# A fourth buffer for the weights' words, an operand zeroed in place, and another order of the first transfers, in a gated linear recurrence with a squared-ReLU network

## The chip, the core and the metric

The kernel runs on one core of a Trainium2 chip. The metric is the device time of one execution in microseconds, the median of several runs. Besides, one execution was recorded by the hardware profiler; all times of single instructions come from that one, and count from the start of its span. A core has five instruction streams that run side by side: PE (TensorE, matrix products), DVE (VectorE), ACT (ScalarE), POOL (GpSimd) and SP (SyncE). Each stream does its instructions strictly in order. SP, ACT and POOL can also issue DMA transfers between memory and the on-chip SBUF; the transfers share 16 DMA engines.

## What is computed

Two stages. The first is a gated recurrence with a complex gate for each of 4 sequences, 8 heads, 768 steps and head size 48; its output, regrouped to 3072 tokens of 384 numbers, goes through a two-layer network with squared ReLU.

```
mag = sqrt(a_re^2 + a_im^2);  scale = min(mag, 0.999) / (mag + 1e-6)
for t in range(S):
    new_re = ar * S_re - ai * S_im
    new_im = ar * S_im + ai * S_re
    S_re, S_im = new_re + outer(k[t], v[t]), new_im
    y[t] = q[t] @ S_re
h = maximum(x @ w_in, 0)          # x: y as (3072, 384); w_in: 384 x 2048
out = (h * h) @ w_out             # w_out: 2048 x 384
```

The weights w_in and w_out are stored as 64-bit floats, and the kernel itself turns them into 32-bit floats on the chip.

## The kernel before

The 3072 tokens are cut into 24 chunks of 128, and two chunks of different sequences form a group: 12 groups. For each group the kernel

- loads gates, queries and keys (`load_parts`, L492 to L511) into the one tile `raw` and the values (`load_values`, L518) into two of the four tiles `vt`. For each chunk b and each half hh of the partitions, `load_parts` issues one large transfer of the rows of three of the four head pairs (L503), and two or three small ones for the fourth pair, whose rows are spread over the 16 partitions that are left (L511; called gap transfers here);
- makes the operands (`make_operands`, 23 steps written o*group*.*step*). Steps 0 and 3 to 11 normalise the gate: o.0 squares (ACT), o.3 their sum (DVE), o.4 and o.5 inverse root and its square (ACT), o.7 a correction (DVE), o.8 to o.10 three scaled copies (ACT), o.11 the gates (DVE, L751 to L755). o.1 and o.2 copy the gate into `ab`, o.6 copies the queries. Step 22 (`grown_squared`, ACT, L764 to L767) and step 13 (`grow`, DVE, L771) form the running product of the gate's growth with a scan; the scan's second operand, `begun`, is a tile of zeros with six columns filled in. Then come the block steps 15 to 17, carries 18 and 19, the products 20, and 21, six small transfers from SBUF to SBUF (`last`);
- forms scores, state and outputs of chunk 0 (steps a*group*.*k*) and chunk 1 (b*group*.*k*), with PE, ACT and DVE. a.1 to a.4 turn the keys (PE) and copy them to `kt` (ACT), a.0 are the scores, a.5 the mask, a.6 the product with the values, a.8 the sum of keys and values, a.9 the new state;
- runs the two-layer network on the group (F, H, X, Y, Z, Q, R), and stores it (s).

Beside the first groups the weights are fetched in 16 blocks of 768 KB, eight of w_in and eight of w_out: f*i* issues the first half of block i on SP and j*i* the second half on POOL (blocks of w_out come whole, on SP), into one of three `words` buffers. D*i* decodes a block on DVE (five instructions, L587 to L596) and W*i* watches its range on ACT (two activations with their sums, L600 to L602). A buffer is free for the fetch three blocks on when D and W have read it. The three sums of the second weight (t0 to t2) take their place in the same ring later.

The order of the work on every engine is written out by hand: the string FRONT (L1072) is gone through token by token, and each token puts its instructions at the end of the streams that they belong to. So a token's place orders it against the others on the same stream alone: l0.0 (gates of group 0), v0, v1 (values of groups 0 and 1), f0, l0.1 (queries and keys of group 0, first half of the partitions; i0.1 the second, on POOL), f1, f2, ... stand in this order on SP. M0 loads ACT's table, M1 makes the mask from the tile `plain` on ACT and PE.

Ahead of FRONT, POOL sets constants: `ident`, `plain`, and zeros in the ends of `vt`, in `qk`, `last`, `prod`, the states, `kt` and `begun`.

Of the kernel before, what the change touches and what calls it, by code (L numbers as in the profile page):

```python
# [21 lines left out]
F32 = mybir.dt.float32  # L22
BF16 = mybir.dt.bfloat16
I32 = mybir.dt.int32
U32 = mybir.dt.uint32
AF = mybir.ActivationFunctionType
ALU = mybir.AluOpType
PSUM = bass.MemoryType.PSUM

P = 128  # L30
# [14 lines left out]
def gap_rows(hh, d):  # L45
    return slice(hh * ROWS + d, (hh + 1) * ROWS)
# [18 lines left out]
def w2_view(w):  # L65
    return w.rearrange("(fb p) m -> p fb m", p=P)
# [359 lines left out]
def quotient_path(ctx, tc, feat, vtok, w_in, w_out, w1, w2, out, n_seq, count):  # L426

    nc = tc.nc
    N, _, D, _, NP, C = feat.shape
    DM, FF = w_in.shape  # L430
# [6 lines left out]
    NFB = FF // P  # L437
    SEG = GC * NG
    E = SEG * C
    L = 8  # L440
    NB = C // L
    W = C + 2
# [4 lines left out]
    const = ctx.enter_context(tc.tile_pool(name="const", bufs=1))  # L447
    dec = ctx.enter_context(tc.tile_pool(name="dec", bufs=1))
    nrm = ctx.enter_context(tc.tile_pool(name="nrm", bufs=1))
    tmp = ctx.enter_context(tc.tile_pool(name="tmp", bufs=1))  # L450
# [10 lines left out]
    def rows(hh):  # L461
        return head_rows(hh, D)
# [7 lines left out]
    def pads(hh):  # L470
        return gap_rows(hh, D)
# [7 lines left out]
    def tt(out, in0, in1, op):  # L479
        nc.vector.tensor_tensor(out=out, in0=in0, in1=in1, op=op)  # L480
# [2 lines left out]
    raw = const.tile([P, 4, GC, NG, C], F32, name="raw")  # L483

    vt = [const.tile([C, DM + PAD], F32, name=f"vt{i}") for i in range(2 * GC)]
    for t in vt:
        nc.gpsimd.memset(t[:, DM:], 0.0)


    TWO_QUEUES = 3  # L490
# [1 line left out]
    def load_parts(gi, part=None, second=False):  # L492


        parts = [slice(A_RE, Q), slice(Q, V), slice(A_RE, V)][2 if part is None else part]
        queues = [nc.sync, nc.scalar if part == 0 else other if gi < TWO_QUEUES else nc.sync]
        if part != 0 and gi < TWO_QUEUES:
            queues[not second] = None
        for b, n in enumerate(groups[gi]):
            for hh, queue in enumerate(queues):  # L500
                if queue is None:
                    continue
                queue.dma_start(  # L503
                    out=raw[rows(hh), parts, b].rearrange("d x g t -> d x (g t)"),
                    in_=feat[n, hh, :, parts, 0:NG].rearrange("d x g t -> d x (g t)"))

                gap = raw[pads(hh), parts, b]
                rest = feat[n, hh].rearrange("(r g) x p t -> r x g p t", g=NG)[:, parts, :, NG]
                for i in range(min(gap.shape[1:3])):
                    at = (slice(None), i) if gap.shape[1] < NG else (slice(None), slice(None), i)  # L510
                    queue.dma_start(out=gap[at], in_=rest[at])  # L511
# [15 lines left out]
    nc.vector.memset(ones, 1.0)  # L527

    mask = const.tile([C, C], F32, name="mask")
    plain = const.tile([C, C], F32, name="plain")  # L530
    nc.gpsimd.memset(plain, 1.0)
    nc.gpsimd.affine_select(out=plain, in_=plain, pattern=[[-1, C]], compare_op=ALU.is_ge, fill=0.0,
                            base=0, channel_multiplier=1)
# [1 line left out]
    def turn_mask(step):  # L535
        if step == 0:

            nc.scalar.activation(out=sums[:, 0:1], in_=tiny, func=AF.Abs_reciprocal_sqrt)
            return
        nc.scalar.copy(out=mask.rearrange("p (j n) -> p n j", j=L),  # L540
                       in_=plain.rearrange("p (n j) -> p n j", j=L))
        turned = pm.tile([C, C], F32, tag="m", name="turned")
        nc.tensor.transpose(turned, mask, ident)
        nc.scalar.copy(out=mask.rearrange("p (j n) -> p n j", j=L),
                       in_=turned.rearrange("p (n j) -> p n j", j=L))
# [8 lines left out]
    qk_of = [const.tile([P, 4, GC, NG, W], F32, name=f"qk{i}") for i in range(2)]  # L554
    last = [const.tile([P, 4, GC, W], F32, name=f"last{i}") for i in range(2)]
    prod = [const.tile([P, 3, GC, NP], F32, name=f"prod{i}") for i in range(2)]
    for t in qk_of:
        nc.gpsimd.memset(t[:, :, :, :, C:W], 0.0)

    states = [[const.tile([P, 2, NP, ROWS], F32, name=f"state{b}{i}") for i in range(2)]  # L560
              for b in range(GC)]
    for t in last + prod + states[0] + states[1]:
        nc.gpsimd.memset(t, 0.0)
    kt = [const.tile([C, NP, P], F32, name=f"kt{i}") for i in range(2)]
    for t in kt:
        nc.gpsimd.memset(t, 0.0)

    sums = const.tile([P, NGR], F32, name="sums")
    ends = const.tile([P, NGR, SEG], F32, name="ends")
    begun = const.tile([P, E], F32, name="begun")  # L570
    nc.gpsimd.memset(begun, 0.0)
    sizes = const.tile([P, 2, 2 * NBLK], F32, name="sizes")
    nc.vector.memset(sizes, 1.0)
    tiny = const.tile([P, 1], F32, name="tiny")
# [30 lines left out]
    words_of = {}  # L605

    def block(i):

        return order[i] == "2", order[:i].count(order[i])

    def fetch(i, second=False):
        of_w2, j = block(i)
        f, fbs = slice(j * BLK, (j + 1) * BLK), slice(j * 2, (j + 1) * 2)
        if (w_out if of_w2 else w_in).dtype == F32:
            if second:
                return
            if of_w2:
                nc.sync.dma_start(out=w2[:, fbs], in_=w2_view(w_out)[:, fbs])
            else:
                for at, gs, src in w1_views(w_in, D, crossed=True):  # L620
                    nc.sync.dma_start(out=w1[at, gs, f], in_=src[:, :, f])
            return
        if i not in words_of:
            words_of[i] = dec.tile([P, E, 2], I32, name="words", bufs=3)
        words = words_of[i]
        if of_w2:
            nc.sync.dma_start(out=words.rearrange("p (k m) w -> p k (m w)", k=2),
                              in_=w2_view(w_out)[:, fbs].bitcast(I32))
        else:
            for at, gs, src in w1_views(w_in, D, crossed=True):  # L630
                if (at.start >= ROWS) != second:
                    continue
                (other if second else nc.sync).dma_start(
                    out=words[at].rearrange("p (g f) w -> p g (f w)", g=NG)[:, gs],
                    in_=src[:, :, f].bitcast(I32))
# [13 lines left out]
    def sum_weights(i):  # L649
        x, y = ((half[0][1], half[0][0]), (half[1][1], w2_sums[0] if i else None),  # L650
                (half[1][0], w2_sums[1] if i > 1 else None), (half[1][1], half[0][1]))[i]
        w2_sums.append(half[0][1] if i == 3 else
                       dec.tile([P, NFB // 2, DM // 2], F32, tag="words", name="w2_sum", bufs=3))
        tt(w2_sums[i], x, y, ALU.subtract)

    def factor(z):
# [17 lines left out]
    def make_operands(gi):  # L674
# [4 lines left out]
        tiles = {}  # L679
# [81 lines left out]


        def grown_squared():
            nc.scalar.activation(out=tiles["sq"][:, 0], in_=tiles["sq"][:, 1], func=AF.Square)  # L764
            at = tiles["sq"][:, 0].rearrange("p (s t) -> p s t", s=SEG)[:, :, 0]
            nc.scalar.copy(out=begun.rearrange("p (s t) -> p s t", s=SEG)[:, :, 0], in_=at)
            nc.scalar.mul(out=at, in_=at, mul=0.0)  # L767

        def grow():
            u, v = tiles["sq"][:, 0], tiles["sq"][:, 1]  # L770
            nc.vector.tensor_tensor_scan(out=v, data0=u, data1=begun, initial=0.0, op0=ALU.mult,  # L771
                                         op1=ALU.add)
            tt(r[:, K], r[:, K], v, ALU.mult)

# [267 lines left out]
    def outputs(i, r):  # L1042
# [27 lines left out]


    FRONT = (  # L1072
        "l0.0 M0 j0 v0 v1 f0 o0.0 l0.1 i0.1 o0.3 o0.1 o0.4 o0.5 o0.7 o0.2 M1 o0.8 D0 f1 j1 o0.9 "
        "o0.10 o0.6 o0.11 f2 j2 W0 W1 D1 o0.22 f3 j3 o0.12 W2 o0.13 o0.15 o0.14 f4 j4 W3 l1 i1 "
        "o0.16 W4 o0.17 D2 o0.18 o1.6 o0.19 f5 j5 o0.20 o1.0 W5 a0.1 o1.3 o0.21 o1.1 D3 a0.2 "
        "a0.3 o1.4 a0.4 a0.8 o1.5 o1.2 o1.7 f6 j6 b0.0 a0.9 o1.8 b0.1 b0.5 o1.9 b0.6 D4 b0.2 "
        "b0.3 b0.7 a0.0 b0.4 o1.10 W6 b0.8 o1.11 f7 j7 a0.5 o1.12 o1.22 a0.6 b0.9 o1.13 W7 v2 "
        "a0.7 o1.15 o1.14 g0 l2 i2 o1.16 F0.0 o1.17 F0.1 H0.0 D5 o1.18 F0.2 H0.1 o2.6 o1.19 f8 "
        "F0.3 H0.2 F0.4 H0.3 o1.20 o2.0 F0.5 H0.4 W8 a1.1 o2.3 o1.21 D6 a1.2 a1.3 o2.1 a1.4 "
        "a1.8 o2.4 o2.2 F0.6 D7 f9 H0.5 o2.5 a1.0 H0.6 a1.9 F0.7 a1.5 W9 f10 o2.7 a1.6 b1.1 "  # L1080
        "a1.7 D8 b1.0 o2.10 o2.8 H0.7 b1.5 o2.9 f11 b1.6 D9 b1.2 b1.3 b1.7 T0.0 b1.4 g1 W10 "
        "o2.11 T0.1 W11 f12 F1.0 D10 o2.12 o2.22 F1.1 H1.0 D11 T0.2 H1.1 f13 W12 F1.2 o2.15 "
# [61 lines left out]
    def ranges(step):  # L1144
# [33 lines left out]
        "R": outputs,  # L1178
        "s": store,
        "f": fetch,  # L1180
        "j": lambda i: fetch(i, True),
        "i": lambda gi, part=None: load_parts(gi, part, True),
        "D": weights,
        "W": lambda i: watch(words_of[i], i) if i in words_of else None,
        "t": sum_weights,
        "l": load_parts,
        "v": load_values,
        "M": turn_mask,
        "K": ranges,
    }  # L1190
# [65 lines left out]
```

## Time and profile before

| | |
|---|---|
| time, median of 5 runs | 707.14 us (705.84 to 707.90) |
| the profiled execution | 706.8 us, its span 705.1 us |
| PE busy | 618.9 us (88%) |
| DVE busy | 524.2 us (74%) |
| ACT busy | 386.2 us (55%) |
| POOL busy | 36.1 us (5%) |
| mean granted TensorE clock | 0.986 |
| moved by DMA | 47.75 MB |
| chain that ended last | PE 75%, DVE 14%, DMA 4%, ACT 3% |

The table's shares are means over the whole span. The page also cuts the span into 40 slices of 17.6 us and gives the busy share of each in tenths; there the start looks unlike the rest:

```profile
PE   0006489999889999999999999999999999999995
...
DVE  1899999999699786896785885995986976972120
...
DMA  6973634461333063061151051151240330110101
```

PE does nothing in the first three slices, about 53 us; DVE is almost empty in the first slice only; DMA is busiest in the second. The chain "that ended last" is followed backwards from the last instruction: at each step to what released it. SPq in a row is a transfer being issued by SP, and DMA a transfer under way.

### The profile page before, as it was taken

The page shows a single profiled execution, that of the slowest core. Times are in us where ns is not written, and L with a number is a line of the kernel's source. Part 1 is how long each engine was busy: PE and PEld are TensorE (multiplying, and loading weights), DVE is VectorE, ACT ScalarE, POOL GpSimd, SP SyncE. Part 2 cuts the span into 40 slices and gives each one's busy share as a digit, 9 for nine tenths or more (in the row PEclk, how much of TensorE's full clock was granted, in tenths as well). Part 3 has the DMA queues.
Part 4 walks back from the last instruction along what each step waited for, and adds up shares of the span by engine and source line. Part 5 has one row for each costly group of instructions (what it writes and reads, how often), then busy time and mean ns, then how long its engine had stood idle before and what let it go on. Part 6 is the DMA issues. An engine that isn't in the chain of part 4 may idle for free.

```text
span 705.1 us, 12510 instructions
## 1 busy us (share of the span) xinstructions
PE 618.9 (88%) x4955; PEld 544.4 (77%) x4955; DVE 524.2 (74%) x916; ACT 386.2 (55%) x684; POOL 36.1 (5%) x91
## 2 busy tenths in 40 slices
PE   0006489999889999999999999999999999999995
PEld 0005377776578898998999989989989989989895
DVE  1899999999699786896785885995986976972120
ACT  6638487754648547537457557366476476440330
POOL 6331200000000000000000000000000000000000
PEclk9999699999999999999999999999999999999999
DMA  6973634461333063061151051151240330110101
GB/s 166 191 136 70 143 78 144 143 111 43 68 74 64 6 94 71 2 125 39 29 113 23 29 113 24 52 94 20 75 80 11 84 77 5 29 23 2 29 1 28
DMA packets 44164, 47.75 MB, mean 68 GB/s; under 512 B 6016, under 2 KB 39104, under 8 KB 44096
## 3 DMA queue, kind: packets, MB, share of 16 engines
q1 hardware_dynamic: 41408, 41.35, 27.9%
q0 software_dynamic: 2208, 5.11, 3.7%
q8 instruction: 41, 0.67, 0.4%
q10 hardware_dynamic: 480, 0.39, 0.2%
q14 instruction: 27, 0.22, 0.1%
HBM read 36.18 MB, written 4.72 MB: 58 GB/s over the span
## 4 chain that ended last, share of the span: by engine, by line
PE 75%; DVE 14%; DMA 4%; ACT 3%; SPq 2%; issue 1%; DVEq 0%; ACTq 0%
PE h_ps L961 30%; PE o_ps L1038 26%; PE a_ps L872 7%; PE y L898 3%; DMA words<-in_moe_w_in_dram 3%; PE y L864 3%; PE add L919 3%; DVE pr L480 2%; DVE ab L480 2%; PE tp L879 2%; DVE room L480 1%; PE o_ps L977 1%; DVE qk L480 1%; DVE decoded L589 1%; DVE decoded L594 1%
## 5 line engine op out<-in xcount | busy, mean ns | idle before, releaser
L961 PE MATMUL h_ps<-x,w 128*128 128x256 f32 x1152 | 257.5, 384 | 6.8 <-DMA x<-x 6.8
L961 PEld LDWEIGHTS h_ps<-x,w 128*128 128x128 f32 x1152 | 220.3, 193 | 37.9 <-issue 6.0
L966 ACT ACTIVATE h<-h_ps 128x512 f32<-128x512 f32 x96 | 57.5, 599 | 103.7 <-PE h_ps L961 95.8
L1038 PE MATMUL o_ps<-w,h 128*128 128x192 f32 x640 | 111.1, 328 | 0.0
L1038 PEld LDWEIGHTS o_ps<-w,h 128*128 128x128 f32 x640 | 103.6, 190 | 1.8 <-issue 0.9
L480 DVE TENSOR_TENSOR pr<-ab 128x384 f32<-128x384 f32 (+2 forms) x168 | 66.4, 413 | 4.4 <-ACT ab L759 0.5
L967 ACT ACTIVATE h<-h 128x512 f32<-128x512 f32 x96 | 60.6, 631 | 3.0
L879 PE MATMUL tp<-ident,qk 128*128 128x128 f32 x120 | 22.0, 294 | 44.6 <-DVE qk L480 42.7
L480 DVE TENSOR_TENSOR a<-a_ps,mask 128x1024 f32<-128x1024 f32 x24 | 29.4, 1223 | 38.4 <-PE a_ps L872 38.4
L480 DVE TENSOR_TENSOR mix<-h 128x256 f32<-128x256 f32 x40 | 16.9, 421 | 53.7 <-ACT h L967 53.7
L1038 PE MATMUL o_ps<-w_sum,mix 128*128 128x192 f32 x320 | 55.9, 328 | 0.0
L1038 PEld LDWEIGHTS o_ps<-w_sum,mix 128*128 128x128 f32 x320 | 52.0, 190 | 1.1 <-DVE state L480 0.7
L879 PEld LDWEIGHTS tp<-ident,qk 128*128 128x128 f32 x120 | 13.6, 145 | 50.6 <-issue 43.8
L480 DVE TENSOR_TENSOR ab<-pr 128x192 f32<-128x192 f32 (+1 forms) x180 | 45.8, 276 | 4.6
L685 ACT ACTIVATE qk<-raw 128x768 f32<-128x768 f32 x24 | 36.7, 1531 | 16.3 <-DVE raw L480 8.8
L480 DVE TENSOR_TENSOR qk<-ab,qk 128x768 f32<-128x768 f32 x48 | 44.9, 956 | 0.9
L977 PE MATMUL o_ps<-w,h 128*128 128x384 f32 x128 | 42.3, 488 | 0.0
L872 PE MATMUL a_ps<-qk 48*128 48x128 f32 x576 | 39.8, 286 | 0.0
L872 PEld LDWEIGHTS a_ps<-qk 48*128 48x128 f32 x576 | 35.2, 193 | 4.2 <-issue 4.2
L685 ACT ACTIVATE ab<-raw 128x768 f32<-128x768 f32 x24 | 37.1, 1562 | 2.3 <-DVE qk L480 2.3
L480 DVE TENSOR_TENSOR room<-ab,carry 128x1344 f32<-128x1344 f32 x24 | 36.2, 1551 | 2.2 <-ACT carry L800 2.2
L977 PEld LDWEIGHTS o_ps<-w,h 128*128 128x128 f32 x128 | 24.1, 190 | 16.2 <-DVE w L480 0.7
(106 smaller groups left out, 804.3 us busy)
## 6 DMA issues: line engine op xcount, KB each, us to landing
raw<-in_feat_dram SPq DMA_DIRECT2D x40, 288.0 KB
words<-in_moe_w_out_dram SPq DMA_DIRECT2D x8, 768.0 KB
last<-qk SPq DMA_DIRECT2D x72, 64.5 KB
vt<-in_vtok_dram SPq DMA_DIRECT2D x24, 192.0 KB
out_dram<-o SPq DMA_DIRECT2D x24, 192.0 KB
raw<-in_feat_dram SPq DMA_DIRECT2D x120, 32.0 KB
words<-in_moe_w_in_dram POOLq DMA_DIRECT2D x8, 192.0 KB, 4.9
words<-in_moe_w_in_dram SPq DMA_DIRECT2D x8, 192.0 KB
```

Source lines behind the costliest of these rows:

```text
L480: nc.vector.tensor_tensor(out=out, in0=in0, in1=in1, op=op)
L685: nc.scalar.activation(out=out.rearrange("p c j n -> p c n j"), func=AF.Copy, in_=in_.rearrange("p c (n j) -> p c n j", j=L), **kwargs)
L864: nc.tensor.matmul(ys[p_ % 2][crossed(hh, p_), p_ // 2], lhsT=states[b][1 - c_seq % 2][rows(hh), c, p_], rhs=operand(c, p_, rows(hh)), sta ...
L872: nc.tensor.matmul(ps[:, hh, p_], lhsT=operand(2 + c, p_, rows(hh)), rhs=operand(c, p_, rows(hh)), start=(c == RE), stop=(c == IM))
L879: nc.tensor.transpose(tp[:, g], operands[gi][:, 2 + c, b, g, 0:C], ident)
L898: nc.tensor.matmul(tiles["y"][p_ % 2][crossed(hh, p_), p_ // 2], lhsT=v[:, at:at + ROWS], rhs=tiles["am"][:, hh, p_], start=(first and p_ ...
L919: nc.tensor.matmul(add[rr, c, p_], lhsT=kt[c][:, p_, rr], rhs=v[:, at:at + D], start=True, stop=True)
L961: nc.tensor.matmul(ps[:, j], lhsT=w1[:, g, (2 * f + j) * P:(2 * f + j + 1) * P], rhs=x_of[i][:, g], start=(g == 0), stop=(g == NG - 1))
L966: nc.scalar.activation(out=h, in_=h_ps[i, f], func=AF.Relu)
L967: nc.scalar.activation(out=h, in_=h, func=AF.Square)
L977: nc.tensor.matmul(o_of[i, b], lhsT=tokens_of(i, f, b)[:, j], rhs=w2[:, k], start=(k == 0), stop=(k == NFB - 1))
L1038: nc.tensor.matmul(to, lhsT=x(k)[:, j], rhs=factor(z)[:, 2 * k + j], start=(z in (0, 1, 3) and k == j == 0), stop=(k == KH // 2 - 1 and j ...
```

## The change

Five edits.

1. The ring of `words` (and of the weight sums) gets four buffers instead of three. Room for it comes from `begun`, which is no longer a tile of its own, and from `plain`, which now lies in the tile of the temporary `pr`.
2. `grown_squared` takes a half of the group's own tile `room` (`both[:, 0]`, read last by the gates) as `begun`. So POOL zeroes it once for every group, between the gates (L754) and ACT's copy into it (L766).
3. POOL's zeros for `qk`, `last`, `vt`, `kt`, `prod` and the states move from the start to a token M2, which stands on POOL between j1 and j2.
4. In l0.0 the gap transfers of chunk 1 (two that were SP's, two that were ACT's) go to POOL's queue.
5. FRONT's start changes. On SP the blocks 0, 1 and 2 now come ahead of the values: l0.0, f0, l0.1, f1, f2, v0, f3, v1, f4 instead of l0.0, v0, v1, f0, l0.1, f1, f2, f3, f4. Further on, o1.5 moves ahead of a0.4, and b0.2 ahead of b0.5 and o1.9.

```diff
-    for t in vt:
-        nc.gpsimd.memset(t[:, DM:], 0.0)
...
+                if part == 0 and b:
+                    queue = nc.gpsimd
                 gap = raw[pads(hh), parts, b]
...
-    plain = const.tile([C, C], F32, name="plain")
+    plain = tmp.tile([P, 4 * NP * D], F32, tag="pr", name="plain")[:, 0:C]
...
+            return
+        if step == 2:
+
+            for t in ([t[:, :, :, :, C:W] for t in qk_of] + last + [t[:, DM:] for t in vt]
+                      + kt + prod + states[0] + states[1]):
+                nc.gpsimd.memset(t, 0.0)
             return
...
-    begun = const.tile([P, E], F32, name="begun")
-    nc.gpsimd.memset(begun, 0.0)
...
-            words_of[i] = dec.tile([P, E, 2], I32, name="words", bufs=3)
+            words_of[i] = dec.tile([P, E, 2], I32, name="words", bufs=4)
...
-                       dec.tile([P, NFB // 2, DM // 2], F32, tag="words", name="w2_sum", bufs=3))
+                       dec.tile([P, NFB // 2, DM // 2], F32, tag="words", name="w2_sum", bufs=4))
...
         def grown_squared():
+            begun = tiles["both"][:, 0]
+            nc.gpsimd.memset(begun, 0.0)
...
-            nc.vector.tensor_tensor_scan(out=v, data0=u, data1=begun, initial=0.0, op0=ALU.mult,
+            nc.vector.tensor_tensor_scan(out=v, data0=u, data1=tiles["both"][:, 0], initial=0.0, op0=ALU.mult,
...
-        "l0.0 M0 j0 v0 v1 f0 o0.0 l0.1 i0.1 o0.3 o0.1 o0.4 o0.5 o0.7 o0.2 M1 o0.8 D0 f1 j1 o0.9 "
-        "o0.10 o0.6 o0.11 f2 j2 W0 W1 D1 o0.22 f3 j3 o0.12 W2 o0.13 o0.15 o0.14 f4 j4 W3 l1 i1 "
-        "o0.16 W4 o0.17 D2 o0.18 o1.6 o0.19 f5 j5 o0.20 o1.0 W5 a0.1 o1.3 o0.21 o1.1 D3 a0.2 "
-        "a0.3 o1.4 a0.4 a0.8 o1.5 o1.2 o1.7 f6 j6 b0.0 a0.9 o1.8 b0.1 b0.5 o1.9 b0.6 D4 b0.2 "
-        "b0.3 b0.7 a0.0 b0.4 o1.10 W6 b0.8 o1.11 f7 j7 a0.5 o1.12 o1.22 a0.6 b0.9 o1.13 W7 v2 "
+        "l0.0 M0 f0 j0 l0.1 i0.1 f1 j1 M2 f2 j2 v0 o0.0 o0.3 o0.1 o0.4 o0.5 o0.7 o0.2 M1 o0.8 "
+        "D0 o0.9 o0.10 o0.6 o0.11 W0 W1 D1 o0.22 f3 v1 j3 o0.12 W2 o0.13 o0.15 o0.14 f4 j4 W3 "
+        "l1 i1 o0.16 W4 o0.17 D2 o0.18 o1.6 o0.19 f5 j5 o0.20 o1.0 W5 a0.1 o1.3 o0.21 o1.1 D3 "
+        "a0.2 a0.3 o1.4 o1.5 a0.4 a0.8 o1.2 o1.7 f6 j6 b0.0 a0.9 o1.8 b0.1 b0.2 b0.5 o1.9 b0.6 "
+        "D4 b0.3 b0.7 a0.0 b0.4 o1.10 W6 b0.8 o1.11 f7 j7 a0.5 o1.12 o1.22 a0.6 b0.9 o1.13 W7 "
```

## The prediction

> **What bounds the kernel now.** I read the profile from coarse to fine: busy time by stretch first, then the chain of waits, then the timelines of the engine the chain names and of the queues that feed it. Busy time by stretch (columns: stretch in us, its length, PE, weight load, DVE, ACT, POOL, granted clock, DMA share, GB/s):
>
> ```profile
> 0.00:20.00 20.00, 0.48 (x1) 0.18 (x1) 4.69 (x10) 11.27 (x13) 14.61 (x40) 1.00 0.72 174
> 20.00:40.00 20.00, 0.00 (x0) 0.00 (x0) 18.91 (x28) 14.50 (x27) 7.80 (x15) 1.00 0.96 177
> 60.00:80.00 20.00, 12.03 (x166) 10.59 (x164) 18.95 (x23) 14.85 (x28) 4.07 (x8) 0.86 0.43 99
> 300.00:400.00 100.00, 100.00 (x795) 91.39 (x794) 75.13 (x140) 57.70 (x100) 0.37 (x2) 1.00 0.31 58
> ```
>
> There are two regimes. From about 190 us PE is full and sets the time. Before that VectorE is full: 76.3 of the 80 us from 20 to 100. Only the first 20 us have an idle VectorE (4.69 us busy), and there DMA is the busy resource. So a microsecond of that idle time removed reaches the end, if the DVE order behind it can move forward as a block. VectorE's timeline (start, duration, line, what it does, idle time before it and what ended that):
>
> ```profile
> 8.71 0.96 DVE L713 SCALAR_TENSOR_TENSOR room<-room 128x768 f32<-128x768 f32 x1 [7.22 <-ACT room L700]
> 12.74 0.96 DVE L731 SCALAR_TENSOR_TENSOR z<-room,z 128x768 f32<-128x768 f32 x1
> 18.69 0.56 DVE L587 TENSOR_SCALAR decoded<-words 128x768 int32<-128x768 int32 x1 [4.99 <-DMA words<-in_moe_w_in_dram]
> 26.68 0.56 DVE L587 TENSOR_SCALAR decoded<-words 128x768 int32<-128x768 int32 x1 [0.33 <-DMA words<-in_moe_w_in_dram]
> ```
>
> VectorE is free at 13.70 and waits 4.99 us for the words of weight block 0 (D0); those of block 1 (D1) cost another 0.33. The chain of waits agrees: it is a stack of weight transfers until the scan of group 0.
>
> ```profile
> 8.31 9.34 DMA words<-in_moe_w_in_dram
> 17.66 5.19 DMA words<-in_moe_w_in_dram
> 22.85 0.95 ACT size L600 x2
> 24.18 5.92 DMA words<-in_moe_w_in_dram
> 30.74 1.76 DVE room L771
> ```
>
> The third line is the buffer limit: the fourth fetch waits until ACT's watch (L600) has read the first buffer. What stands ahead of block 0 on SP's queue:
>
> ```profile
> 5.07 2.70 SPq L520 DMA_DIRECT2D vt<-in_vtok_dram  x4
> 7.81 1.58 SPq L633 DMA_DIRECT2D words<-in_moe_w_in_dram  x3
> 9.45 0.57 SPq L503 DMA_DIRECT2D raw<-in_feat_dram  x1
> ```
>
> Four value tiles, 768 KB, go first, and they are first read at 59.81 (PE add, L919).
>
> **Part 1: values behind weights.** The two-microsecond stretches from 8 to 30 us moved 164 to 253 GB/s, mean 203. One unit of 768 KB (the gates of group 0; one weight block; queries and keys of group 0; the four value tiles) is then 3.9 us. First packets come at 2.1. After the change block 0 is the second unit instead of the third: 2.1 + 2 x 3.9 = 9.9, or 11.8 if half a unit of queries and keys is served in between. Block 1 becomes the fourth: 17.7 to 19.6, against 26.68 now.
>
> **Part 2: four gap transfers to POOL, its memsets behind.** ACT and SP lose two 24 KB issues each, POOL gains four. ACT's queue issues now end at 5.31; the table load (1.28) and first activation (0.20) then end at 6.83, and the squares start at 7.19. Without the two issues (its last remaining one ends at 3.21) ACT is free at about 4.8. POOL is free for DMA once its select on plain ends (1.90; about 1.75 without four vt memsets). Now it issues at 7.37 because it zeroes for 5.5 us first:
>
> ```profile
> 6.69 0.76 POOL L571 MEMSET begun<- 128x768 f32 x1
> 7.37 1.80 POOL L633 DMA_DIRECT2D words<-in_moe_w_in_dram  x3
> ```
>
> The first packet of that issue is at 9.26 in the trace's packet records, 1.9 us later. Four issues of 0.51 from 1.75, the last at 3.3, put the last packets near 5.6 and the squares at about 5.9: 1.3 earlier. Bounds: 5.5 (the row transfers of the second sequence land at 5.2), and 10.6 if POOL's transfers took the 8.8 us from issue to landing that its longest raw transfer took in a full queue. I take 5.9, since these queues are empty. The Trainium skill speaks against this move: "DMA: Bandwidth & Descriptors", section Specifications, gives a first byte after about 1 us on the software path and 0.6 on the hardware path. The rows here say 1.9 for POOL and 1.76 for ACT (0.81 to 2.57). By the page's difference the squares would be 0.4 later than on a hardware queue, by the rows 0.1; both are less than what the earlier issue gains.
>
> **Part 3: the sum to D1.** From squares to the end of L731 it takes 13.70 - 7.19 = 6.5 on ACT and DVE. D0 then starts at 5.9 + 6.5 = 12.4, its words being there since 11.8. D0 takes 4.1 (18.69 to 22.83), the gates 3.6 (22.74 to 26.36, L751 to L755): D1 at 20.1, its words there at 19.6. 26.68 - 20.1 = **6.6 us earlier**. ACT keeps up: its three activations before the gates end at 5.9 + 10.4 = 16.3, queries 17.8 (their data the third unit, 13.8 to 15.7), two watches of 1.85 end at 21.5, squares and copies of L764 to L767 at 22.9; D1 ends at 24.3, when the scan wants them.
>
> **Part 4: the scan's operand zeroed in place.** Per group one POOL memset of 0.76 (row of begun) is added, which waits for the gates' multiply (L754) and which ACT's copy (L766) waits for. Behind it on POOL stand block 3's second half (group 0) or nothing urgent; behind L766 on ACT, the whole activation order. Cover: in group 1 L754 ends at 72.93 and L766 starts at 74.70, 1.77 us; near 394 it is 3.2. 0.76 fits: cost 0. Upper bound: POOL's copy L924 takes 0.19 alone and 0.65 beside a busy DVE, 3.4 times; 2.6 would stall ACT by 0.8 in group 1, and the 1.2 us from the end of L767 (75.14) to DVE's scan (76.36) would hide that. The skill's "SBUF — State Buffer", section Who interferes with whom, says a DVE instruction in a two-port mode locks POOL out for its length, but one with two inputs only hinders a POOL instruction that reads; a memset doesn't. By that rule only the 0.56 us tensor_scalars could hold it: 1.3 at most, still covered.
>
> **Part 5: the fourth buffer.** No DVE instruction after D1 waits for words in this profile, so the later fetches' gain is nothing by itself; it keeps them off the path when everything moves up. What it cannot do is move more bytes: the raw tiles of group 1 queue behind blocks 2 to 4 and the values as before. They land at 47.4, and the DMA idle ahead of them (rows 6:8, 16:18 and 34:36 at 95, 159 and 90 GB/s) is worth 2.6 us: 44.8 at best. ACT's queries of group 1 (1.54) then end at 46.3, squares (1.48) 47.8, the watch of block 5 (2.04) 49.8, where L685 of ab is due at 55.96 - 6.6 = 49.4. **Cost 0.4.** The last two weight-sum buffers and the plain tile's new home cost nothing: their earlier users end long before (plain's last reader at 13.4, the first pr at 33.39).
>
> **Part 6: two swaps in ACT's order.** o1.5 now precedes a0.4:
>
> ```profile
> 59.04 0.48 ACT L883 COPY kt<-tp 128x384 f32<-128x384 f32 x1 [0.30 <-PE tp L879]
> 59.41 0.30 ACT L884 COPY kt<-tp 128x96 f32<-128x96 f32 x1
> 59.55 0.86 ACT L722 ACTIVATE room<-z 128x768 f32<-128x768 f32 x1
> ```
>
> The copies start when L722 is done, 0.6 later; the chain runs from them over PE's add and a_ps to DVE's mask at 65.00, which already waits for PE: **cost 0.6**. Bounds: 0 if PE is early by then, 0.9 (the whole L722). b0.2 before o1.9 makes ACT wait 1.2 for PE, but the gates that use o1.9 are 5 us away: 0.
>
> Sum: 6.6 - 0.4 - 0.6 = 5.6 us off the DVE block, carried to 188 us because DVE's later waits up to there, 10.0 us for a_ps the largest, are for PE and ACT, which move with it, and then through the PE regime unchanged. The profiled execution took 706.8 (span 705.1 and 1.7 around it), 0.3 under the median: 701.2 for it, **701.5** for the median of 707.14.
>
> **The rivals.** *The gain is capped at group 1* (chance 0.20). With four buffers SP sends block 5 straight behind its half of group 1's raw tiles, and half a unit (1.9 us) is served among POOL's half. Raw lands at 46.7, queries end 48.2, squares 49.7, watch 51.7, 2.3 later than due: 6.6 - 2.3 - 0.6 = 3.7, so 703.4. For it: DMA is at 1.0 from 18 to 34 and 36 to 44. Against: SP's half is ahead in its own queue. *The gate gaps come late through POOL* (0.03): squares at 10.6, D0 at 17.1, D1 at 24.8, gain 1.9 less 0.6: 705.8, not to be told from no change. *It does not do what it says* (0.03): block 0's words still end DVE's wait near 18, as POOL's half has its own queue; 706 to 708. Against: the chain holds SP's half for the late one. *Slower* (0.12): the moved memsets stand on POOL between j1 and j2, and the new memset of the scan's operand behind both. If POOL issues j1 as late as now (about 18.7), 5.5 us of memsets end at 24.2, j2 at 25.8, operand 26.6, ACT's two copies 27.0; the scan at 27.0 still gains 3.7. If the memsets stretch beside a busy DVE, each microsecond goes to the scan: from 9.2 us (1.7 times) it is slower; at twice, 11 us and 1.5 for the operand, the scan starts at 33.2 instead of 30.74: 709.6. For it: L924's 0.65. Against: that one reads, a memset only writes.
>
> **How the numbers follow.** The forecast has 0.62, 699 to 703. Its low end is no cost in parts 5 and 6 and squares at 5.5 (7.0 gained: 700.1), and another 1.2 where PE's half clock at 105 to 108 us (3.8 us for twelve matmuls of L961 that take 2.6 otherwise) falls elsewhere: 698.9. Upwards I go to 706.5, past the cap and the late gaps. What a measurement of this kernel tells from no change is 0.2%, 1.4 us. Faster: 0.62 + 0.20 = 0.82, same 0.03 + 0.03 = 0.06, slower 0.12.
>
> **What would show it.** Squares near 5.9; D0 at 12 to 13 without a wait for words; D1 near 20; vt issued behind three weight blocks; POOL's memset between L754 and L766 in all 12 groups with ACT not waiting there; DVE's products of group 0 near 46. It is wrong if L771 of group 0 starts after 27, or if ACT waits for raw past 46.

## The result and the profile after

| | before | after |
|---|---|---|
| time, median | 707.56 us (705.48 to 710.40, 64 runs) | 706.18 us (704.78 to 708.08, 34 runs) |
| ratio, 95% interval | 1 | 0.9979 (0.9972 to 0.9985) |
| the profiled execution | 706.8 us, span 705.1 us | 706.17 us, span 704.5 us |
| mean granted TensorE clock | 0.986 | 0.989 |
| PE, DVE, ACT, POOL busy | 618.9, 524.2, 386.2, 36.1 us | 624.3, 527.7, 386.5, 46.6 us |

The change makes the kernel 0.21% faster, 1.5 us by the ratio, where 5.6 us were forecast. 701.5 was the forecast, 706.18 the time.

Line numbers shift by about two in the kernel after: the first instruction of a decode is L585 (L587 before), its next ones L587, L589 and L592, the squares L698, the inverse root's correction L729, the gates L749 to L753. The new zeros are L544 (M2) and L763 (the scan's operand).

Busy time by stretch after the change, the same rows as shown of before (stretch, its length, PE, weight load, DVE, ACT, POOL, granted clock, DMA share, GB/s):

```profile
0.00:20.00 20.00, 0.47 (x1) 0.18 (x1) 9.91 (x12) 13.95 (x17) 16.28 (x43) 1.00 0.90 204
20.00:40.00 20.00, 0.00 (x0) 0.00 (x0) 19.13 (x35) 12.24 (x24) 8.75 (x16) 1.00 0.84 167
60.00:80.00 20.00, 15.08 (x138) 12.93 (x134) 17.82 (x24) 13.91 (x25) 4.88 (x10) 1.00 0.47 92
300.00:400.00 100.00, 100.00 (x795) 91.41 (x794) 75.16 (x139) 57.22 (x98) 1.85 (x4) 1.00 0.30 58
```

The first row reads like a success: VectorE's busy time went from 4.69 to 9.91 us, DMA's share from 0.72 to 0.90. Yet it has only two instructions more, 12 instead of 10. Two decode instructions should take 1.5 us (0.56 and 0.96 before), not 5.2. Busy time isn't work done, as VectorE's timeline after the change shows:

```profile
12.45 0.96 DVE L729 SCALAR_TENSOR_TENSOR z<-room,z 128x768 f32<-128x768 f32 x1
13.33 4.17 DVE L585 TENSOR_SCALAR decoded<-words 128x768 int32<-128x768 int32 x1
17.53 0.96 DVE L587 SCALAR_TENSOR_TENSOR decoded<-words,decoded 128x768 int32<-128x768 int32 x1
24.52 0.55 DVE L585 TENSOR_SCALAR decoded<-words 128x768 int32<-128x768 int32 x1
28.56 1.75 DVE L771 TENSOR_TENSOR_SCAN room<-room 128x768 f32<-128x768 f32 x1
```

The wait of 4.99 us for words is gone: D0 starts 5.36 us earlier (13.33 instead of 18.69). The words came early enough: by the trace's signals of landed transfers the last of block 0's six transfers had landed at 10.73, the last of block 1's at 17.71. But D0's first instruction takes 4.17 us; the same one takes 0.55 in D1, and took 0.56 before. 3.6 of the 5.36 us are lost in a single instruction. Over the same time POOL's timeline has the zeros of M2:

```profile
11.95 0.23 POOL L544 MEMSET qk<- 128x48 f32 x2
12.09 1.89 POOL L544 MEMSET last<- 128x1040 f32 x2
...
14.09 1.01 POOL L544 MEMSET kt<- 128x512 f32 x2
...
15.13 1.94 POOL L544 MEMSET state<- 128x512 f32 x4
17.00 1.62 POOL L631 DMA_DIRECT2D words<-in_moe_w_in_dram  x3
23.86 0.74 POOL L763 MEMSET room<- 128x768 f32 x1 [5.23 <-DVE ab L480]
```

The last zero ends at 17.07, VectorE's instruction at 17.50, 0.43 us later: nearly its own normal length. It looks as though it stood still until POOL was done. The zeros themselves aren't stretched (5.12 us from 11.95 to 17.07). The chain of waits has it too, in the place where DMA stood before:

```profile
3.89 4.82 DMA words<-in_moe_w_in_dram
...
8.98 4.30 DMA raw<-in_feat_dram
...
13.33 4.18 DVE decoded L585
```

How the lead over the profile of before runs on, each from the start of the same VectorE instruction in both: 5.36 us at D0; 2.16 at D1 (26.68 to 24.52); 2.18 at the scan of group 0 (30.74 to 28.56) and still 2.17 at 61.74, where group 1 begins; 1.09 at the first mask product (65.00 to 63.91); 0.70 at the third (113.47 to 112.77); 0.67 at 192 us; 0.6 in the spans. So the first loss is the large one, and two smaller ones follow. At the mask product PE's timeline after the change shows why:

```profile
58.20 1.95 PE L919 MATMUL add<-vt,kt 128*64 128x48 f32 x32 [1.36 <-DMA last<-qk]
60.08 2.93 PE L872 MATMUL a_ps<-qk 48*128 48x128 f32 x24
62.80 1.06 PE L872 MATMUL a_ps<-last 48*128 48x128 f32 x8
```

In the profile before, the same three rows were:

```profile
59.81 1.95 PE L919 MATMUL add<-vt,kt 128*64 128x48 f32 x32 [0.81 <-ACT kt L884]
61.69 2.81 PE L872 MATMUL a_ps<-qk 48*128 48x128 f32 x24
64.34 0.61 PE L872 MATMUL a_ps<-last 48*128 48x128 f32 x8
```

PE's add starts 1.61 us earlier than before, not 2.18: ACT's copies of the keys now stand behind L720 (the swap). The releaser named, the transfer `last`, is not the last to come: ACT's copies end at 58.10. And the scores take 3.78 us (60.08 to 63.86) instead of 3.26 (61.69 to 64.95).

### The profile page after: what moved, and what is told of

It is laid out like the page before. It is cut to its first block, busy times and chain, and to the rows that moved or that the text cites. A ratio compares the mean times of both kernels' runs of the same rounds, so it can differ in the third digit from the quotient of the medians.

```text
span 704.5 us, 12547 instructions
## 1 busy us (share of the span) xinstructions
PE 624.3 (89%) x4955; PEld 548.7 (78%) x4955; DVE 527.7 (75%) x916; ACT 386.5 (55%) x684; POOL 46.6 (7%) x106
## 3 DMA queue, kind: packets, MB, share of 16 engines
q1 hardware_dynamic: 41280, 41.30, 27.7%
q0 software_dynamic: 2336, 5.21, 3.8%
## 4 chain that ended last, share of the span: by engine, by line
PE 75%; DVE 14%; DMA 4%; ACT 2%; SPq 2%; issue 1%; POOL 1%; DVEq 0%; POOLq 0%
PE h_ps L961 32%; PE o_ps L1038 26%; PE a_ps L872 6%; PE y L898 3%; PE y L864 3%; PE add L919 2%; DVE ab L480 2%; DMA raw<-in_feat_dram 2%; PE tp L879 2%; DMA words<-in_moe_w_in_dram 2%; DVE pr L480 1%; DVE room L480 1%; PE o_ps L977 1%; DVE decoded L585 1%; DVE qk L480 1%; SPq L831 1%
## 5 line engine op out<-in xcount | busy, mean ns | idle before, releaser
L872 PE MATMUL a_ps<-qk 48*128 48x128 f32 x576 | 41.3, 293 | 0.0
```

The costliest lines, as they stand in the source:

```text
L872: nc.tensor.matmul(ps[:, hh, p_], lhsT=operand(2 + c, p_, rows(hh)), rhs=operand(c, p_, rows(hh)), start=(c == RE), stop=(c == IM))
```

## The experiments

The runs below move, double or undo parts of the change. Theory A: POOL's zeros, back to back, hold VectorE's tensor_scalar until they end; all else of the change works as it should. Rivals: the words are not really there at 13.3; the stretch is the price of DMA traffic; the gap transfers, the fourth buffer or the swaps take the gain. All runs were compared with the kernel before on the same chip (median of before 707.46, 707.50 and 707.09 us in three sessions). "after" in an edit is the changed kernel.

| run | median us | ratio to before, 95% |
|---|---|---|
| after | 706.18 | 0.9979 (0.9972 to 0.9985) |
| e1_zeros_on_dve | 703.73 | 0.9954 (0.9936 to 0.9972) |
| e2_zeros_late | 703.17 | 0.9937 (0.9917 to 0.9957) |
| e3_zeros_twice | 705.99 | 0.9985 (0.9968 to 1.0001) |
| e4_order_only | 704.24 | 0.9957 (0.9939 to 0.9975) |
| e5_late_old_act_order | 702.23 | 0.9930 (0.9912 to 0.9948) |
| e6_late_gaps_hw | 707.45 | 1.0000 (0.9985 to 1.0015) |
| e7_late_three_buffers | 702.97 | 0.9936 (0.9914 to 0.9958) |
| e8_zeros_beside_d2 | 705.56 | 0.9967 (0.9945 to 0.9988) |
| e10_zeros_first_gaps_hw | 706.53 | 0.9983 (0.9967 to 1.0000) |
| e11_dve_zeros_old_act_order | 702.33 | 0.9932 (0.9908 to 0.9956) |
| e12_smallest_edit | 701.71 | 0.9925 (0.9900 to 0.9949) |

### e1: the zeros on VectorE

```diff
                       + kt + prod + states[0] + states[1]):
-                nc.gpsimd.memset(t, 0.0)
+                nc.vector.memset(t, 0.0)
```

> The changed kernel, with the zeros of M2 (qk, last, vt, kt, prod, states) written by DVE, idle there until 8.4 us, instead of POOL. Theory A (POOL's zeroing from 11.95 to 17.07 holds DVE's first decode instruction, L585, which took 4.17 us instead of 0.56): L585 of block 0 takes 0.56, D0 ends near 17.5 instead of 21.0, the scan of group 0 (L771) starts near 25.2 instead of 28.56, and the time falls by about 3 us from the changed kernel's 706.2, to 703. Theory B (the 4.17 us are a late arrival of block 0's words, or DMA traffic): L585 stays above 3 us and the time within 1 us of 706.2.

Measured: 703.73 us, span 701.2. VectorE zeroes from 1.46 to 7.20, while it would wait for the squares anyway, and its timeline shows D0 unheld:

```profile
13.18 0.55 DVE L585 TENSOR_SCALAR decoded<-words 128x768 int32<-128x768 int32 x1
```

The words were there at 13.18, and the instruction has its old length. The rival of late words falls. So does that of DMA traffic: from 12 to 18 us it was 220 GB/s here and 218 in the changed kernel.

### e2: the zeros on POOL, later

Only M2's place is changed: from behind j1 to behind j4.

```diff
-        "l0.0 M0 f0 j0 l0.1 i0.1 f1 j1 M2 f2 j2 v0 o0.0 ...
-        ... f3 v1 j3 o0.12 W2 o0.13 o0.15 o0.14 f4 j4 W3 "
+        "l0.0 M0 f0 j0 l0.1 i0.1 f1 j1 f2 j2 v0 o0.0 ...
+        ... f3 v1 j3 o0.12 W2 o0.13 o0.15 o0.14 f4 j4 M2 W3 "
```

> The changed kernel, with POOL's zeros of M2 after j4, where DVE does the scan and tensor_tensor operations with no tensor_scalar among them. Theory A in its narrow form (only tensor_scalar instructions are held): L585 0.56, no DVE instruction between 28 and 33 longer than in the changed kernel, scan near 25.2, time near 703. Theory A in a wide form (any DVE instruction is held by POOL's zeroing): the tensor_tensor steps there stretch by up to 5 us in all and the time is back at 706 or above. Theory B: L585 above 3 us, 706.

Measured: 703.17 us, span 700.3. POOL's timeline, the longest of the zeros:

```profile
24.65 1.89 POOL L544 MEMSET last<- 128x1040 f32 x2
...
27.69 1.94 POOL L544 MEMSET state<- 128x512 f32 x4
```

and VectorE's beside them:

```profile
13.67 0.55 DVE L585 TENSOR_SCALAR decoded<-words 128x768 int32<-128x768 int32 x1
...
25.29 1.75 DVE L771 TENSOR_TENSOR_SCAN room<-room 128x768 f32<-128x768 f32 x1
27.07 0.96 DVE L480 TENSOR_TENSOR raw<-raw,room 128x768 f32<-128x768 f32 x1
```

The zeros cost as much on POOL as before, but now stand beside a scan and products of two tensors, and those keep their 1.75 and 0.96 us. So it isn't "POOL busy" that costs, but POOL's zeros beside a tensor_scalar. The scan is 3.27 us earlier than in the changed kernel (28.56 to 25.29), the time 3.0; M2's place is all that differs, so it cost that.

### e3: every zero written twice

```diff
                 nc.gpsimd.memset(t, 0.0)
+                nc.gpsimd.memset(t, 0.0)
```

> The changed kernel, with each memset of M2 done twice: 5.1 us more on POOL. Theory A: L585 of block 0 grows from 4.17 to about 9.3 us, or the hold breaks between two memsets; the scan starts near 33.7 and the time is some 5 us above the changed kernel, 711. Theory B: L585 stays near 4.2; POOL is later, but the second half of block 2 has cover until 41, so the time stays near 706.

Measured: 705.99 us, not to be told from the changed kernel's 706.18, where twice the hold would have made it slower than before. VectorE's timeline:

```profile
13.15 0.65 DVE L586 TENSOR_SCALAR decoded<-words 128x768 int32<-128x768 int32 x1
...
14.84 1.36 DVE L590 TENSOR_SCALAR decoded<-decoded 128x768 int32<-128x768 int32 x1
...
29.29 1.76 DVE L772 TENSOR_TENSOR_SCAN room<-room 128x768 f32<-128x768 f32 x1 [2.97 <-ACT room L768]
```

and POOL's, where L545 is the second writing:

```profile
13.53 1.24 POOL L544 MEMSET last<- 128x1040 f32 x1
14.82 0.96 POOL L545 MEMSET last<- 128x1040 f32 x1
15.73 1.37 POOL L544 MEMSET last<- 128x1040 f32 x1
...
27.95 0.76 POOL L764 MEMSET room<- 128x768 f32 x1
```

The miss teaches more than a hit would have. A second zero into the same tile waits for the first and leaves about 0.06 us between them, and VectorE gets in there: L586 takes 0.65, and now it is POOL's zeros that are stretched (1.24 and 1.37 instead of 0.96). L590, begun just after a zero, waits for that one zero: 1.36. So the hold goes both ways, whoever started first keeping the other out; what made it 3.6 us in the changed kernel is that independent zeros follow each other without a gap. The scan's loss here is another one: POOL, in order, comes to the scan's operand only at 27.95, and ACT and VectorE wait for it (2.97 us). That is the mechanism of the prediction's slower rival, with the zeros at twice the work instead of twice the time.

### e4: the kernel before, with the values behind the weights

All other edits undone.

```diff
-        "l0.0 M0 j0 v0 v1 f0 o0.0 l0.1 i0.1 ... f2 j2 W0 W1 D1 o0.22 f3 j3
+        "l0.0 M0 j0 f0 o0.0 l0.1 i0.1 ... f2 j2 v0 W0 W1 D1 o0.22 f3 v1 j3
```

> The kernel before with one part of the change: v0 behind f2 and v1 behind f3 on SP; three buffers, zeros at the start and gap transfers as before. If the order of the values alone is the gain: squares at 7.2, D0 at 13.7 to 14, L587 0.56 as POOL has done its zeroing by 7.4, D1 near 21.5, time 4 to 5 us below the kernel before, 703. If the second halves on POOL, issued from 7.4, hold block 0 until 16 or later: D0 at 16 to 17 and 705.

Measured: 704.24 us, 3 us faster than before and 2 faster than the whole change. VectorE's timeline:

```profile
13.84 0.56 DVE L587 TENSOR_SCALAR decoded<-words 128x768 int32<-128x768 int32 x1 [0.31 <-DMA words<-in_moe_w_in_dram]
...
21.99 0.56 DVE L587 TENSOR_SCALAR decoded<-words 128x768 int32<-128x768 int32 x1 [0.48 <-issue]
...
26.04 1.75 DVE L771 TENSOR_TENSOR_SCAN room<-room,begun 128x768 f32<-128x768 f32 x1
```

The reordering on SP alone gives 4.7 us at the scan. Ahead of D0 0.31 us of waiting for words is left, ahead of D1 0.48 us for which the profile names no releaser; POOL still zeroes first and issues its halves from 7.37. Not all of the 4.7 arrives: VectorE waits 0.84 us for ACT's carries at 43.70, and at the first mask product the lead is 3.2 (65.00 to 61.78).

### e5 and e11: the swaps in ACT's order undone

e5 is e2, e11 is e1, each with o1.5 behind a0.8 and b0.2 behind D4 again.

```diff
-        "a0.2 a0.3 o1.4 o1.5 a0.4 a0.8 o1.2 ... b0.1 b0.2 b0.5 o1.9 b0.6 D4 b0.3
+        "a0.2 a0.3 o1.4 a0.4 a0.8 o1.5 o1.2 ... b0.1 b0.5 o1.9 b0.6 D4 b0.2 b0.3
```

> The kernel of e2 (zeros after j4), with the two swaps in ACT's order undone (a0.4 ahead of o1.5 again, b0.2 back behind D4). Theory: of e2's 5.4 us at the inverse of group 1, 0.5 was lost at the first mask, since a0.4 stood behind o1.5 and PE's add waits for it; undone, add starts 0.6 earlier against DVE, the first mask waits some 0.4 instead of 0.93, and the time falls by 0.5 to about 702.7. Rival (the loss there is PE's clock alone, not the order): the mask waits as long as in e2 or e1, time within 0.3 of e2.

> The kernel of e1 (zeros on DVE, idle at the start), with the two swaps in ACT's order undone. e5 showed that undoing them starts PE's add 0.54 earlier. Theory: the time is 0.5 to 1 below e1's 703.7, 702.7 to 703.2, as e5 is 0.9 below e2. Rival (PE's slow matmuls between 55 and 70 decide, not the order): the time stays within 0.3 of e1.

Measured: 702.23 us (e5; e2 703.17) and 702.33 (e11; e1 703.73). PE's timeline of e5:

```profile
54.39 1.95 PE L919 MATMUL add<-vt,kt 128*64 128x48 f32 x32 [0.81 <-ACT kt L884]
```

In e2 the same add starts at 54.93, with 1.36 us idle before it instead of 0.81. The swap costs 0.54 us there, as the prediction said (0.6). Whether that reaches VectorE, the profiles of e2 and e5 don't show: the first mask product starts at 60.10 in both, since PE's scores took 0.5 us longer in e5's. In the profiles of e1 and e11 they took equally long, and there VectorE waits 0.56 us less for them in e11. Its timeline in e1:

```profile
60.13 1.23 DVE L480 TENSOR_TENSOR a<-a_ps,mask 128x1024 f32<-128x1024 f32 x1 [1.44 <-PE a_ps L872]
```

and in e11, where D0 began 0.69 us later:

```profile
60.23 1.22 DVE L480 TENSOR_TENSOR a<-a_ps,mask 128x1024 f32<-128x1024 f32 x1 [0.88 <-PE a_ps L872]
```

Both pairs of times agree in sign, 0.9 and 1.4 us; the intervals of their ratios overlap, so the size at the end is known only roughly.

### e6 and e10: the gap transfers back on SP and ACT

e6 is e2 without the move of the four gap transfers. e10 is the same, with the zeros put ahead of j0.

```diff
-                if part == 0 and b:
-                    queue = nc.gpsimd
                 gap = raw[pads(hh), parts, b]
```

> The kernel of e2, with the four gap transfers of chunk 1 back on SP and ACT. In e1, e2 and the changed kernel the squares began at 6.75 to 7.24, not at the predicted 5.9, against 7.19 before. Theory (the move gave nothing, since a transfer on POOL lands as late as the later issue on SP and ACT): squares at 6.9 to 7.4, time within 0.5 of e2's 703.2. Rival (the move gives what was predicted, and something else ate it): squares at 8.0 or later, time about 704.4.

> The kernel of e6 (gap transfers on SP and ACT), with M2's zeros ahead of j0 on POOL again. In e6 the squares began at 12.05, because POOL, with neither zeros nor gap transfers in front, issued j0 at 1.68 and its packets shared the DMA engines with the small gap transfers (the last of them ended at 9.2 and 10.3). Theory (what helps the gates is that POOL's large transfers start late, whether zeros or gap transfers hold them back): j0 is issued near 6.8, squares near 7.2 again, D0 at 13.7 to 14.2 with L585's place at 0.56, time near 703.5. Rival (the gap transfers are slow on SP and ACT in this order for another reason, block 0's first half behind them on SP): squares at 10 or later and 706 or more.

Measured: 707.45 us (e6) and 706.53 (e10). ACT's timeline of e6:

```profile
12.05 1.48 ACT L696 ACTIVATE room<-raw 128x1536 f32<-128x1536 f32 x1 [5.16 <-DMA words<-in_moe_w_in_dram]
```

POOL's of e6:

```profile
1.68 1.80 POOL L629 DMA_DIRECT2D words<-in_moe_w_in_dram  x3
```

ACT's of e10:

```profile
7.00 1.48 ACT L696 ACTIVATE room<-raw 128x1536 f32<-128x1536 f32 x1
```

In e6 POOL, with nothing to do first, issues its half of weight block 0 at 1.68, and the small gap transfers on SP's and ACT's queues come late: their last packets end at 8.91 (ACT's queue) and 10.01 (SP's), the signals that they have landed come at 10.95 and 11.83, and the squares start at 12.05 instead of 7.24 in e2. In e10 the zeros hold that issue back to 6.73, the last gap has landed at 6.85, and the squares are at 7.00. The two differ only in the place of the zeros: what POOL issued early delayed the gaps, not the queue that they were on. That it did so by sharing the 16 DMA engines with them is the likely way; no run separates it from others. So the move of the gaps to POOL didn't bring the 1.3 us forecast for it; it keeps POOL's queue in an order in which the weights come behind the gaps. Together with late zeros that is worth 4.8 us at the squares.

e10 was expected near e2 and isn't. VectorE's timeline of e10:

```profile
13.48 0.56 DVE L583 TENSOR_SCALAR decoded<-words 128x768 int32<-128x768 int32 x1
...
22.20 0.56 DVE L583 TENSOR_SCALAR decoded<-words 128x768 int32<-128x768 int32 x1 [1.06 <-DMA words<-in_moe_w_in_dram]
...
44.87 3.03 DVE L480 TENSOR_TENSOR room<-ab,carry 128x1344 f32<-128x1344 f32 x2 [1.79 <-ACT carry L798]
```

D0 is in time, but what POOL issues first comes 2.8 us later than in e2 (6.73 instead of 3.88 for j0), and block 1 is 1.06 us late. ACT's watch of block 4 starts at 42.56 instead of 36.21, with the carries behind it in ACT's order; why block 4 is that late stays open (POOL issues its half at the same time in both, SP's issue of the other half ends at 29.27 instead of 26.20). In the first 10 us e10 moves 149 GB/s, e2 177. With these two waits the lead over before falls from 5.2 us at D0 to 2.6 where group 1 begins (61.74 to 59.16). e4, which has POOL's zeros first and the gaps on SP and ACT as well, but three buffers, a `begun` of its own and no swaps, has the same two waits at 0.48 and 0.84 us and a median 2.3 us lower, with intervals that overlap a little; which of those edits makes the difference stays open.

### e7: three buffers

e2 with bufs=3 for the words and the weight sums.

> The kernel of e2, with three buffers in the ring of words instead of four. Theory (no DVE instruction waits for words from block 2 on, the buffer is worth little): D0 and D1 as in e2, D2 at 38, time within 0.5 of 703.2. Rival (the buffer holds the DVE block together once it has moved up): a wait for words or for group 1's raw tiles of 1 us or more shows on DVE between 37 and 60, as the 0.84 at the carries in e4, and the time is 704 or more.

Measured: 702.97 us against e2's 703.17: the fourth buffer gives nothing that these runs can tell.

### e8: the zeros beside the third decode

e2 with M2 behind i1 instead of j4.

```diff
-        "l1 i1 o0.16 W4 o0.17 D2
+        "l1 i1 M2 o0.16 W4 o0.17 D2
```

> The kernel of e2, with M2's zeros on POOL behind i1, so that they run from about 35 to 40 and meet D2 (L585 at 37.97 in e2, its words there long before). Theory A, narrow: L585 of block 2 starts near 38 and lasts until POOL's last memset ends, near 40.1, so about 2.5 us instead of 0.56, with no DVE instruction before it stretched; scan of group 1 some 2 us later than in e2, time 705. Theory B (the long L585 of the changed kernel had to do with the words of block 0): L585 of block 2 takes 0.56.

Measured: 705.56 us. VectorE's timeline:

```profile
37.69 2.15 DVE L585 TENSOR_SCALAR decoded<-words 128x768 int32<-128x768 int32 x1
39.87 0.96 DVE L587 SCALAR_TENSOR_TENSOR decoded<-words,decoded 128x768 int32<-128x768 int32 x1
```

POOL's:

```profile
37.47 1.94 POOL L544 MEMSET state<- 128x512 f32 x4
```

This bears theory A out at another place and another time, where nothing waited for words (in e2 the same instruction of D2 took 0.56): the first tensor_scalar that meets the zeros takes 2.15 us and ends at 39.84, again 0.43 after the last zero (39.41). The products beside the earlier zeros (34.3 to 37.4) keep their length.

### e12: the smallest edit

What is left when all that didn't pay is taken out: SP's new order, the four gap transfers on POOL, the zeros behind j4. Three buffers, the old swaps, `begun` a tile of its own, zeroed once by VectorE.

```diff
+    begun = const.tile([P, E], F32, name="begun")
+    nc.vector.memset(begun, 0.0)
...
-            words_of[i] = dec.tile([P, E, 2], I32, name="words", bufs=4)
+            words_of[i] = dec.tile([P, E, 2], I32, name="words", bufs=3)
...
-            begun = tiles["both"][:, 0]
-            nc.gpsimd.memset(begun, 0.0)
...
```

> The kernel of e5 with three buffers and with begun as a tile of its own again (zeroed once, by DVE at the start): of the change only the order of SP's first transfers, the gap transfers on POOL and the moved zeros are left, these after j4. Theory (the fourth buffer and the operand zeroed in place give nothing, as e7 showed for the buffer): D0 near 13.5, scan near 25.2, time within 0.6 of e5's 702.2. Rival (the in-place operand or the buffer is part of the gain): 703.3 or more.

Measured: 701.71 us, the lowest median of all, 5.4 below the kernel before and 4.5 below the changed one; from e5 and e11 it can't be told. VectorE's timeline:

```profile
13.54 0.55 DVE L587 TENSOR_SCALAR decoded<-words 128x768 int32<-128x768 int32 x1
...
25.16 1.75 DVE L771 TENSOR_TENSOR_SCAN room<-room,begun 128x768 f32<-128x768 f32 x1
...
59.07 1.23 DVE L480 TENSOR_TENSOR a<-a_ps,mask 128x1024 f32<-128x1024 f32 x1
```

The scan leads before by 5.6 us, the mask product, without any wait, by 5.9.

## Why the prediction was right in part, and where it failed

**What bounds the start** was read rightly: VectorE's 4.99 us for words was a wait that could be removed, and what VectorE gains there goes to the end. e12's 5.6 us at the scan became 5.4 in span and time.

**Part 1** held: in the changed kernel block 0 had landed at 10.73 (forecast 9.9 to 11.8) and block 1 at 17.71 (17.7 to 19.6), and the order on SP alone gave 3 us (e4).

**The step that failed is in part 3: "D0 takes 4.1 (18.69 to 22.83)".** The duration came from a row of before in which POOL wrote nothing beside D0; in the new order M2 stands there. D0 took 7.7 us (13.33 to 21.07), 3.6 more, all in its first instruction. With squares at 6.91 instead of 5.9, 20.1 + 0.9 + 3.6 makes 24.6 for D1; it came at 24.52. M2's time was within the prediction's reach: its slower rival puts the zeros at 18.7 to 24.2, beside the gates and the D1 that it places at 20.1, and used that only for the question when the scan's operand would be zeroed. (They ran earlier, from 11.95 to 17.07.) The slower rival asked whether a busy VectorE stretches POOL's zeros, and rejected it since a memset only writes. The other direction, POOL first and VectorE held, was never asked, though part 4 draws on the page that has it, for VectorE holding POOL alone. The Trainium skill states it on the page "SBUF — State Buffer", section Who interferes with whom: when a VectorE instruction in a two-port mode (tensor_scalar can be in one) meets GpSimd, whichever began first has the shared ports and the other is blocked altogether. The traces agree: 0.56 us became 4.17 (after) and 2.15 (e8), while POOL kept its length; in e3, with VectorE in first, POOL's 0.96 became 1.37. The page speaks of the length of one instruction; here the hold lasted over a train of them, 3.7 us from 13.33 to 17.07. The prediction's own sign of being wrong, group 0's scan after 27, came true: it started at 28.56.

**Part 2** was mis-sized: squares at 6.91, forecast 5.9. The last packet of POOL's gaps ended at 5.71 (5.6 was estimated), but the signal that they had landed, for which ACT waits, came only at 6.69, 1.0 us later; the estimate had left 0.3 us from the packet to the squares. In the profile before, on ACT's own queue, it was 0.5 (6.52 to 7.04). The prediction's packet times also stand 0.3 us late against its instruction times: it has first packets at 2.1, where busy time by stretch shows no traffic from 1.60 to 1.80 us and 115 GB/s from 1.80 to 2.00; its 1.9 and 1.76 us from issue to first packet are 1.6 and 1.4. What the move is good for, the order against block 0's half, stood in no step of the prediction (e6, e10).

**Part 4** held: L763 ran at 23.86 and 71.98, between the gates, ACT's copies followed without waiting for it in all 12 groups, and e12 without it is no slower or faster than can be told. Only with the zeros doubled did it come late (e3).

**Part 5** was right that the fourth buffer gives nothing by itself (e7). Its cost of 0.4 didn't show, and neither did the rival that caps the gain at group 1: ACT's queries of group 1 ran at 45.98 after the change, and VectorE waited for nothing there. With a lead of only 2.2 us that tests little; but in e2, with 5.4, the queries ran at 44.42, and VectorE waited for nothing from 26 to 57 us either.

**Part 6** held: forecast 0.6, measured 0.57 from 2.18 to 1.61 at the add, 0.54 between e2 and e5 there, and 0.56 less waiting at the mask product between e1 and e11.

**The rest of the lost lead**, 0.5 us at the first mask product and 0.4 at the third, fell where VectorE waits for PE's scores (1.49 us instead of 0.39 at the first, 0.94 instead of 0.57 at the third); at the first, these products took 0.5 us more than in the profile of before. The prediction's range allowed for that only downwards. Its reading that VectorE waits 10.0 us for a_ps up to 188 us is wrong: that is the sum up to 240; up to 188 it is 1.3 us in three waits, and 5.2 at 191.99. The miss doesn't come from there, as that long wait is 5.26 after the change.

So at D1 the forecast lead of 6.6 us lost 0.9 to the squares and 3.6 to the hold, which leaves 2.1; 2.16 was measured. What bounds the start, and the new order, were right; that the sum of 5.6 comes near e12's 5.4 is in part luck: e12 leads by 5.56 at D1 where 6.6 was forecast, and has neither the swaps nor the fourth buffer, for which 1.0 was taken off. 706.18 lies outside 699 to 703, the range of the likeliest case; the upper end of 706.5 was room left for other mechanisms, none of which was the one that decided. The direction held, but barely: 1.5 us, where the prediction took 1.4 as the least that it could tell.

## What to carry to other kernels

When work is moved to another engine or another time, look up what will run beside it in the new place, and ask in both directions who holds whom; a duration from the old profile holds only beside the old neighbours. A VectorE instruction that is suddenly several times its usual length, and ends just after a POOL instruction, as D0's 4.17 us did, may be a wait that the profile books as work. Before keeping a bundle of edits, run its parts alone: here one reordering carried most of the gain, the place of the zeros decided how much of it was kept, and the fourth buffer and the operand zeroed in place carried none that these runs can tell.

## What the runs showed of the hardware that was not expected

- A tensor_scalar on integers is held by POOL's zeros (0.56 to 4.17 us), but a scan (1.75), a product of two tensors (0.96) and a scalar_tensor_tensor (0.96 at 12.45 after the change) beside the same zeros are not stretched at all.
- The four moved transfers of 24 KB take 128 packets more on POOL's queue and 256 fewer on the queues of SP and ACT; the page's queue lines go from 2208 to 2336, and from 41408 and 480 to 41280 and 352.
- PE's eight score products on `last` for the first mask product take 0.61 us in the profiles of before, e2, e3, e8, e10 and e12, and 1.06 in those of after, e1, e4, e5, e6, e7 and e11. The granted clock reads 1.00 in every two microseconds from 54 to 66 us in before and after alike. Why is open; between profiles it moves VectorE by about half a microsecond at the first mask product.
